# Lists of two numbers a token, weights gathered from a table, and list work dealt out by estimated time

## The chip, the cores and the metric

The kernel runs on one core of a Trainium2 chip. The metric is the device time in microseconds (us) of one execution, the median over runs. The engines of the core work side by side, each through its own instructions in order: TensorE (PE, matrix products into PSUM), VectorE (DVE), ScalarE (ACT), GpSimd (POOL), and SyncE (SP), which here issues most of the DMAs. An instruction that waits for a semaphore holds all that stand behind it on its engine.

## The reference

The first half is linear attention with decay over 4 batches, 8 heads, 768 positions and head size 64. Its output, as a matrix x of 3072 tokens by 512, goes through a mixture of 8 experts of which each token takes the two best:

```
logits = x @ w_gate;  noisy = logits + log1p(exp(x @ w_noise)) * noise
top2 = the two largest of noisy (8 experts);  w = softmax over these two
out[token] = sum over its two experts e of  w * (relu(x @ w1[e]) @ w2[e])    # 512 -> 1024 -> 512
```

All is float32.

## The kernel before

**Attention.** A loop over `t` from 0 to 11 takes two chunks of 128 tokens a turn (a stage, "stage t"). In it PE transposes k and q of the next pair (`trans_k`, L297; `trans_q`, L310), makes the state products (`kv`, L385), the outputs of pair t (`intra`, `inter`, L350), transposes earlier outputs (`store_x`, L413), multiplies them with the gate's weights (`products`, L404) and makes the scores of the next pair (`scores`, L338), then the logits (L429). ACT empties most of the PSUM results: kT, qT, xo (`evac_o`), xc (`store_x`) and xp (`products`). DVE makes qTs (L317), the states S (L397) and the masked scores `at` (L341). POOL makes kd (`kdecay`, L326). The PSUM name pS has four slots; a stage takes twelve of them in turn (three for k, two for q, one for kv, two for xc, four for the scores), so the third and fourth of the scores take the slots of the two xc.

**Routing.** The tokens are routed in three groups of eight chunks (`GB`). `gate` finds the two best experts of each token (DVE), `weights` their softmax (POOL, the reciprocal on DVE), `count` counts tokens per expert with small PE products of the one-hot `ob`, and `route` gives each choice a place: a tile number `at` and a row `lo` in it.

**Lists.** For each chunk and choice a list unit holds two one-hot codes: `lo` (128 wide, the row) and `hi` (56 wide, the tile; L577). `loads` multiplies hi by the five numbers that a token carries in `vals` (two for its index, three bfloat16 pieces of its weight; L588). `enlist` multiplies lo by that on PE (L598) and adds the result to `found`: for each expert's tile and row, the token's index and weight. `read_lists` and `decode` turn a part of `found` into `recs` (index and weight), and `gather_rows` fetches rows of x from DRAM by an indirect DMA of POOL (L772).

**Order of the work.** Each engine's order is the order of the program's text. Gate, weights, count, route and parts of the lists are generators in `jobs`; `advance(n)` steps through them, a step counting 1 unless it yields another number, and "step" ends the call. In attention it is called after the state updates (`FILLS`) and at the end of a stage (`FILL`, less `SPLIT` where weights are split). The first six units of two chunks are built outright at the end of a stage, at most two a stage (`firsts`, `UPS`), as soon as their group is routed; the list call follows at the end of the next stage.

**Experts.** For expert 0, tiles of 128 tokens go in three parts of 2, 2 and 3 tiles: GEMM1 over eight blocks f (L797, `gemm1`), evacuated by ACT (relu, L803) and DVE (L807), and GEMM2 per tile (L835, `gemm2`), whose result is multiplied by the token's weight (L850, L847). The lists of groups 1 and 2 are finished inside the first two parts; `MIDS` runs something after 12 of the 24 matmuls of a tile. Weights are loaded by SP to `wst` and split in a high and a low part (`split_w`, ACT L748 and DVE L749). Each expert's results are scattered to the output by POOL (L854), after fetching what an earlier expert wrote there (`gather_prev`, L819).

Of the kernel before, what the change touches and what calls it, by code (L numbers as in the profile page):

```python
# [55 lines left out]
NV = 5  # L56
HOT = 2 * (128 + NTL + NV * NTL)
UPS = 2
# [4 lines left out]
FILL, SPLIT, FILLS = 10, 4, 14  # L63
FILL1 = 4
FILL2 = (7, 7, 7, 3, 3, 3, 3, 3)
# [5 lines left out]
GX = 9  # L71
# [53 lines left out]
def kernel(  # L125
# [16 lines left out]
    x_tok = dram.tile([NTOK, DM], FT, name="x_tok")  # L142
    powd = dram.tile([H, 2, 256], FT, name="powd")
# [93 lines left out]
    nc.gpsimd.iota(iotat, pattern=[[1, NTL]], base=0, channel_multiplier=0, allow_small_or_imprecise_dtypes=True)  # L237
    iotar = consts.tile([128, TS], BF, name="iotar")
    nc.gpsimd.iota(iotar, pattern=[[1, TS]], base=0, channel_multiplier=0, allow_small_or_imprecise_dtypes=True)
    vals = consts.tile([128, NCH, 2, NV], BF, name="vals")  # L240
    nc.gpsimd.iota(vals[:, :, :, 0], pattern=[[1, NCH], [0, 2]], base=-(BIG // TS), channel_multiplier=0,
                   allow_small_or_imprecise_dtypes=True)
    nc.gpsimd.iota(vals[:, :, :, 1], pattern=[[0, NCH], [0, 2]], base=0, channel_multiplier=1,
# [32 lines left out]
    def finish(b):  # L276
        while "done" not in RT.get(b, {}):
            advance(1)
# [153 lines left out]
    def gate(b):  # L432
# [18 lines left out]
        acc = t(fl, "glacc")  # L451
# [8 lines left out]
        nl = t(sh, "nl")  # L460
# [23 lines left out]
    def weights(b):  # L484
# [19 lines left out]
        w = t([128, gs, 2], "ww")  # L504
        v.tensor_copy(w[:, :, 0], s)
        v.tensor_mul(w[:, :, 1], e, s)
        cs = slice(GB[b], GB[b + 1])
        for i in range(2, NV - 1):
            v.tensor_copy(vals[:, cs, :, i], w)
            v.tensor_tensor(vals[:, cs, :, i + 1] if i == NV - 2 else w, w, vals[:, cs, :, i], op=SUB)  # L510

# [12 lines left out]
    def route(b):  # L524
# [24 lines left out]
        v.scalar_tensor_tensor(pp, ei, float(NT * TS), pp, op0=MULT, op1=ADD)
# [4 lines left out]
        v.tensor_scalar(atr, pp, 1.0 / TS, -0.5 + 0.5 / TS, op0=MULT, op1=ADD)  # L554
# [16 lines left out]
    def keys(b, c, n, buf):  # L571
# [3 lines left out]
        for o, io, x in ((lo, iotar, RT[b]["lo"]), (hi, iotat, RT[b]["at"])):  # L575
# [4 lines left out]
            yield  # L580
# [28 lines left out]
    def decode(s, out, n):  # L609
# [36 lines left out]
    def places(b):  # L646
        yield "step"
# [537 lines left out]
```

## Time and profile before

| | us |
|---|---|
| median of 3 runs | 780.5 (779.52 to 782.52) |
| the profiled execution | 778.15 |
| its span, first to last instruction | 776.4 |
| PE busy | 733.4 |
| DVE, ACT, POOL busy | 361.4, 223.0, 235.8 |

The span is the time between the first and the last instruction; the profiled execution takes 1.75 us more. An engine's busy time is no measure of its importance by itself: what counts is which wait ends last before an instruction of PE. PEclk is the clock that PE was granted, as a share of 2.4 GHz; 0.5 is 1.2 GHz.

### The profile page before, as it was taken

To read this page: it belongs to the slowest core of one execution; us is meant where nothing else is said; L and a number is where in the kernel's file an instruction comes from. 1 tells how busy PE (TensorE), PEld (TensorE's weight loads), DVE (VectorE), ACT (ScalarE), POOL (GpSimd) and SP (SyncE) were. 2 spreads that over 40 slices of the span, in tenths; PEclk is the share of its full clock that TensorE was granted. 3 is DMA by queue.
4 is the path that set the end of the run, shared out by engine and by line. 5 is a ranking of instruction groups with operands and counts; after the bars stand their busy time and mean duration, and the time that the engine had idled before them with its cause. 6 is when DMAs were issued, how large, how long until landed. Compare 5 with 4: busy or idle time off the path is not lost. (4 is left out here: it accounts for less than half of the span.)

```text
span 776.4 us, 15432 instructions
## 1 busy us (share of the span) xinstructions
PE 733.4 (94%) x6170; PEld 625.6 (81%) x6170; DVE 361.4 (47%) x820; ACT 223.0 (29%) x381; POOL 235.8 (30%) x383
## 2 busy tenths in 40 slices
PE   6999996969989999999999999999999999999995
PEld 4887885858869889898888888888798888889884
DVE  5555788749643554454235333623352443335210
ACT  0445553423203332133213221422142222314200
POOL 2311431302252344332343343243412433221311
PEclk9899999889989999999999999999999999999998
DMA  8899983319063473534253425333442544240210
GB/s 169 190 275 225 280 202 112 123 49 338 1 160 120 137 197 100 178 113 134 86 151 125 123 75 170 123 110 107 142 144 68 155 137 135 66 136 12 75 41 37
DMA packets 88924, 103.21 MB, mean 133 GB/s; under 512 B 35462, under 2 KB 61574, under 8 KB 88848
## 3 DMA queue, kind: packets, MB, share of 16 engines
q1 hardware_dynamic: 77280, 66.01, 31.8%
q0 software_dynamic: 11568, 36.17, 14.3%
q8 instruction: 50, 0.82, 0.4%
q14 instruction: 26, 0.21, 0.1%
HBM read 77.73 MB, written 25.64 MB: 133 GB/s over the span
## 5 line engine op out<-in xcount | busy, mean ns | idle before, releaser
L797 PE MATMUL pS<-xtl,w1h 128*128 128x512 f32 (+3 forms) x544 | 181.9, 334 | 6.2 <-DVE xtl L784 6.1
L797 PE MATMUL pS<-xth,w1h 128*128 128x512 f32 (+3 forms) x544 | 182.6, 336 | 2.8 <-ACT xth L783 2.5
L797 PE MATMUL pS<-xth,w1l 128*128 128x512 f32 (+3 forms) x544 | 181.5, 334 | 0.0
L807 DVE SCALAR_TENSOR_TENSOR ht<-pS,ht 128x256 fp32r<-128x256 f32 (+3 forms) x176 | 76.7, 455 | 136.3 <-ACT ht L803 134.3
L835 PE MATMUL pO<-w2h,ht 128*128 128x512 f32 x384 | 126.2, 400 | 0.0
L835 PE MATMUL pKV<-w2h,ht 128*128 128x512 f32 x384 | 124.8, 396 | 0.0
L803 ACT ACTIVATE ht<-pS 128x512 fp32r<-128x512 f32 (+3 forms) x136 | 65.8, 484 | 184.7 <-PE pS L797 180.2
L854 POOL DMA_INDIRECT out_dram<-ot,rec x46 | 60.5, 1315 | 186.1 <-DVE ot L847 175.2
L797 PEld LDWEIGHTS pS<-xtl,w1h 128*128 128x128 f32 x544 | 103.8, 191 | 15.4 <-DVE xtl L784 6.8
L797 PEld LDWEIGHTS pS<-xth,w1h 128*128 128x128 f32 x544 | 103.4, 190 | 12.6 <-ACT xth L783 3.3
L797 PEld LDWEIGHTS pS<-xth,w1l 128*128 128x128 f32 x544 | 103.5, 190 | 8.8
L783 ACT ACTIVATE xth<-pS 128x512 fp32r<-128x512 f32 (+2 forms) x53 | 29.9, 573 | 208.6 <-PE pS L781 208.5
L835 PEld LDWEIGHTS pO<-w2h,ht 128*128 128x128 f32 x384 | 72.9, 190 | 15.6
L835 PEld LDWEIGHTS pKV<-w2h,ht 128*128 128x128 f32 x384 | 72.1, 188 | 15.5
L835 PE MATMUL pO<-w2l,ht 128*128 128x512 f32 x192 | 75.7, 394 | 0.0
L835 PE MATMUL pKV<-w2l,ht 128*128 128x512 f32 x192 | 75.1, 391 | 0.0
L819 POOL DMA_INDIRECT pv<-out_dram,rec x46 | 46.8, 1018 | 29.2 <-issue 26.0
L772 POOL DMA_INDIRECT xg<-x_tok,rec x46 | 49.0, 1065 | 17.0 <-issue 16.1
L847 DVE SCALAR_TENSOR_TENSOR ot<-pO,rec,pv 128x512 f32<-128x512 f32 x21 | 15.8, 751 | 81.1 <-PE pO L835 81.1
L847 DVE SCALAR_TENSOR_TENSOR ot<-pKV,rec,pv 128x512 f32<-128x512 f32 x21 | 15.8, 751 | 79.8 <-PE pKV L835 79.8
L326 POOL TENSOR_TENSOR kd<-kt,Mk 128x512 f32<-128x512 f32 x24 | 26.6, 1130 | 77.0 <-PE pR L385 41.4
L749 DVE TENSOR_TENSOR w2l<-wst,w2h 128x1024 fp32r<-128x1024 f32 (+1 forms) x33 | 39.4, 1193 | 13.3 <-ACT w2h L748 13.3
(214 smaller groups left out, 971.8 us busy)
## 6 DMA issues: line engine op xcount, KB each, us to landing
wst<-in_moe_w_dram SPq DMA_DIRECT2D x48, 512.0 KB, 4.0
wst<-in_moe_w_dram SPq DMA_DIRECT2D x32, 256.0 KB, 3.8
kt<-in_k_dram SPq DMA_DIRECT2D x12, 512.0 KB, 5.7
qt<-in_q_dram SPq DMA_DIRECT2D x24, 256.0 KB, 6.4
vt<-in_v_dram SPq DMA_DIRECT2D x12, 512.0 KB, 6.2
x_tok<-xc SPq DMA_DIRECT2D x24, 256.0 KB, 4.3
out_dram<-zero SPq DMA_DIRECT2D x24, 256.0 KB, 4.1
xg<-x_tok,rec POOLq DMA_INDIRECT x46, 4.0
```

The costliest lines, as they stand in the source:

```text
L326: nc.gpsimd.tensor_mul(kd[:, :, s], kt[:, :, s], mask(s, slice(0, HP), slice(C - 1, C)).to_broadcast([128, HP, 2, D]))
L749: nc.vector.tensor_tensor(lo[:, r], st[:, r], hi[:, r].bitcast(FT), op=SUB)
L772: nc.gpsimd.indirect_dma_start(out=XG[t][:size(e, t)], out_offset=None, in_=x_tok[:rows, :], in_offset=bass.IndirectOffsetOnAxis(ap=REC[e, ...
L783: nc.scalar.activation(hi, p, AF.Copy)
L797: nc.tensor.matmul(p, W1[a][d][:, fs], xt(b, cs)[:, d], start=(d == 0 and i == 0), stop=(d == DB - 1 and i == 2))
L803: nc.scalar.activation(ht(e, 0, f, cs), p, AF.Relu)
L807: nc.vector.scalar_tensor_tensor(ht(e, 1, f, c), p[:, r], 0.0, ht(e, 0, f, c).bitcast(FT), op0=OP.max, op1=SUB)
L819: nc.gpsimd.indirect_dma_start(out=PV[t][:size(e, t), :], out_offset=None, in_=out, in_offset=bass.IndirectOffsetOnAxis(ap=REC[e, t][:, 0: ...
L835: nc.tensor.matmul(p, ht(e, a, f, cs), W2[b][f // 2][:, f % 2, :], start=(i == 0), stop=(i == len(terms) - 1))
L847: nc.vector.scalar_tensor_tensor(o, p, w, pv, op0=MULT, op1=ADD)
L854: st = nc.gpsimd.indirect_dma_start(out=out, out_offset=bass.IndirectOffsetOnAxis(ap=REC[e, t][:, 0:1], axis=0), in_=o, in_offset=None, bo ...
```

## The change

A token's list entry becomes two numbers, chunk and row, so `NV` is 2 and a unit is 592 columns a chunk instead of 928. `loads` no longer reads `vals`: DVE writes hi times the chunk number, one instruction a chunk, and ACT writes hi times the row number (`scale=rowf`). `weights` no longer writes three pieces; POOL spreads the two weights over the experts and writes them to a table `wtab` in DRAM (token by expert). `decode` gives a token's index and the place of its weight in the table, and `gather_w`, a new indirect DMA on POOL for each tile, fetches the weights to `WR`. `route` drops three steps.

`advance` now counts estimated microseconds: a step counts `OPUS` = 0.21 unless it yields its own estimate. All allowances change. The units are no longer built outright: `build(early(b))` is a job behind `routing(b)`, four units for group 0 (four buffers `HB`) and two for group 1. The first tiles' lists are read as soon as group 0 is listed, not at t = 9. In expert 0, the lists of group 1 are called one block earlier (f = 5), and the counting of group 2 is moved from the middle of tile 1's GEMM2 to the end of tile 0's.

```diff
-NV = 5
+NV = 2
...
-FILL, SPLIT, FILLS = 10, 4, 14
-FILL1 = 4
-FILL2 = (7, 7, 7, 3, 3, 3, 3, 3)
+OPUS = 0.21
+FILL, SPLIT, FILLS = 2.0, 1.2, 3.4
+FILL1, FILLG = 0.9, 4.6
...
-                n -= j or 1
+                n -= j or OPUS
...
             v.max(mx[:, c, :], nl[:, c, :])
-            yield
+            yield 0.1
...
             v.max_index(mi[:, c, :], mx[:, c, :], nl[:, c, :])
-            yield
+            yield 0.15
...
-        w = t([128, gs, 2], "ww")
-        v.tensor_copy(w[:, :, 0], s)
-        v.tensor_mul(w[:, :, 1], e, s)
...
+        wd = t([128, 2, gs, E], "wd")
+        v.tensor_mul(e, e, s)
+        for i, w in enumerate((s, e)):
+            v.tensor_mul(wd[:, i], r["oh"][:, i], w[:, :, None].to_broadcast(sh))
+        v.tensor_add(wd[:, 0], wd[:, 0], wd[:, 1])
+        nc.gpsimd.dma_start(wtab.rearrange("(p c) o -> p (c o)", p=128)[:, GB[b] * E:GB[b + 1] * E],
+                            wd[:, 0].rearrange("p c e -> p (c e)"))
...
-            yield
+            yield 0.0012 * 2 * n * k + 0.08
...
-        v = nc.vector
         _, hi, mv = hot(buf, n)
-        sh = [128, 2 * n, NV, NTL]
-        g = GB[b] + c
-        v.tensor_tensor(mv.rearrange("p k (w j) -> p k w j", w=NV), hi[:, :, None, :].to_broadcast(sh),
-                        vals[:, g:g + n].rearrange("p c r w -> p (c r) w")[:, :, :, None].to_broadcast(sh), op=MULT)
+        mv = mv.rearrange("p k (w j) -> p k w j", w=NV)
+        nc.scalar.activation(mv[:, :, 1, :], hi, AF.Copy, scale=rowf)
+        for i in range(n):
+            k = slice(2 * i, 2 * i + 2)
+            nc.vector.tensor_scalar(mv[:, k, 0, :], hi[:, k, :], float(GB[b] + c + i - BIG // TS), None, op0=MULT)
...
+    def gather_w(e, t):
+        n = size(e, t)
+        nc.gpsimd.indirect_dma_start(
+            out=WR[e % 3][:n, t:t + 1], out_offset=None, in_=wtab,
...
     def build(some):
-        for unit in some:
-            yield from keys(*unit)
-            loads(*unit)
-            yield
+        for b, c, n, buf in some:
+            yield from keys(b, c, n, buf)
+            loads(b, c, n, buf)
+            built.append((b, c, n, buf))
+            yield 0.36
+
+    def early(b):
+
+        return [(b, 2 * i, 2, x) for i, x in enumerate(HB[:4 if not b else 2])]
...
         if 2 * t in GB[1:]:
-            jobs.append(routing(GB.index(2 * t) - 1))
+            b = GB.index(2 * t) - 1
+            jobs.extend((routing(b), build(early(b))))
...
-        while len(built) < UPS and firsts and "done" in RT.get(firsts[0][0], {}):
-            b, c = firsts.pop(0)
-            built.append((b, c, 2, HB[c // 2 % 2]))
-            for _ in build(built[-1:]):
-                pass
-        if t == GX:
-            assert RT[0]["listed"] == GM
+        if RT.get(0, {}).get("listed") == GM and not REC:
             read_lists(0, PARTS0[0])
             load_rec(0)
             for j in range(PARTS0[0]):
                 gather_rows(0, j, GB[1] * C)
+                gather_w(0, j)
...
-    MIDS = {1: lambda: advance(1), 2: lists_done}
+    MIDS = {2: lists_done}
...
-                if f == 6:
+                if f == 5:
                     enlist(units[1])
...
-            advance(50)
+            advance(FILLG)
...
             gemm2(0, t, MIDS.get(t))
+            if t == 0:
+                finish(2, "gated")
+                advance(FILLG)
...
                         gather_prev(e, f)
+                        gather_w(e, f)
```

## Rows read from the trace of the kernel before

**Rows 1.** The head of the page: busy us, share of the span and instructions.

```profile
PE 733.4 (94%) x6170; PEld 625.6 (81%) x6170; DVE 361.4 (47%) x820; ACT 223.0 (29%) x381; POOL 235.8 (30%) x383
```

**Rows 2.** Busy time by stretch, cut at the starts of the attention stages t = 7, 8, 9, 10 and at later points; columns: stretch, its length, busy us of PE, PEld, DVE, ACT and POOL, granted clock, DMA share, GB/s.

```profile
97.80:107.97 10.17, 10.17 (x238) 9.01 (x235) 7.21 (x25) 6.03 (x11) 3.28 (x8) 1.00 0.81 196
107.97:122.39 14.42, 11.43 (x266) 9.90 (x266) 12.19 (x19) 5.20 (x10) 2.78 (x2) 1.00 0.85 231
122.39:141.29 18.90, 13.91 (x267) 11.83 (x266) 16.72 (x45) 6.35 (x11) 3.14 (x2) 0.82 0.17 57
141.29:151.23 9.94, 9.94 (x234) 8.85 (x233) 8.28 (x43) 6.03 (x11) 5.38 (x16) 1.00 0.35 110
151.23:166.94 15.71, 7.05 (x135) 5.28 (x134) 11.30 (x27) 4.75 (x9) 3.64 (x13) 0.90 0.18 67
166.94:196.88 29.94, 28.29 (x187) 25.45 (x188) 18.56 (x83) 7.46 (x17) 5.94 (x20) 0.94 0.68 246
196.88:231.11 34.23, 29.26 (x181) 25.14 (x180) 20.91 (x53) 5.63 (x13) 11.27 (x19) 0.95 0.29 78
231.11:770.00 538.89, 536.04 (x2760) 456.32 (x2760) 207.65 (x346) 142.02 (x227) 174.22 (x248) 1.00 0.38 116
```

**Rows 3.** PE's waits over the whole span: what waited, for whom, total us, times, longest.

```profile
PE pS L797 <- DVE xtl L784: 6.1, 2, 5.7
PE pS L413 <- DVE qTs L317: 3.4, 1, 3.4
...
PE pR L404 <- DVE S L397: 2.2, 1, 2.2
PE pL L598 <- DVE wst L588: 2.2, 2, 2.0
...
PE pL L598 <- DVE l L439: 1.4, 1, 1.4
...
PE pS L338 <- ACT xc L415: 0.8, 2, 0.5
```

**Rows 4.** DVE's timeline at the end of stage t = 7 (start us, us, what), two list units and the qTs behind them; the last row is POOL's at that time.

```profile
109.64 0.68 DVE L577 TENSOR_TENSOR hb<-iotar,lo 128x512 bf16<-128x512 bf16 x1
110.24 0.38 DVE L577 TENSOR_TENSOR hb<-iotat,at 128x224 bf16<-128x224 bf16 x1
110.73 1.32 DVE L588 TENSOR_TENSOR hb<-hb,vals 128x1120 bf16<-128x1120 bf16 x1
111.97 1.54 DVE L577 TENSOR_TENSOR hb<-iotar,lo 128x512 bf16<-128x512 bf16 x1
113.43 1.23 DVE L577 TENSOR_TENSOR hb<-iotat,at 128x224 bf16<-128x224 bf16 x1
...
115.94 0.68 DVE L317 TENSOR_TENSOR qTs<-pS,QS 128x512 f32<-128x512 f32 x1
...
111.64 2.78 POOL L326 TENSOR_TENSOR kd<-kt,Mk 128x512 f32<-128x512 f32 x2 [3.83 <-issue]
```

**Rows 5.** Timelines of stage t = 7: DVE's last routing instruction, then ACT, then PE's scores.

```profile
103.98 0.20 DVE L502 RECIPROCAL ws<-ws 128x8 f32<-128x8 f32 x1
...
103.51 0.60 ACT L372 ACTIVATE xo<-pO 128x512 f32<-128x512 f32 x1 [2.18 <-PE pO L350]
...
104.48 1.09 ACT L415 ACTIVATE xc<-pS 128x512 f32<-128x512 f32 x2
105.44 0.41 ACT L406 ACTIVATE xp<-pR 128x256 f32<-128x256 f32 x1
...
104.97 2.06 PE L338 MATMUL pS<-qT,kT 64*64 64x128 f32 x63
```

**Rows 6.** The end of attention: DVE's weight split and the low part of expert 0's first rows, ACT's high part, and PE.

```profile
159.87 1.23 DVE L749 TENSOR_TENSOR w2l<-wst,w2h 128x1024 fp32r<-128x1024 f32 x1 [1.89 <-ACT w2h L748]
...
165.61 1.28 DVE L784 TENSOR_TENSOR xtl<-pS,xth 128x512 fp32r<-128x512 f32 x2
...
159.73 1.09 ACT L783 ACTIVATE xth<-pS 128x512 fp32r<-128x512 f32 x2
...
166.94 0.58 PE L797 MATMUL pS<-xtl,w1h 128*128 128x256 f32 x1 [5.69 <-DVE xtl L784]
```

**Rows 7.** The first part of expert 0: ACT's first evacuation, and DVE's last gate instruction of group 2.

```profile
174.65 0.66 ACT L803 ACTIVATE ht<-pS 128x256 fp32r<-128x256 f32 x2 [2.44 <-DMA x_tok<-xc]
...
193.22 0.23 DVE L480 TENSOR_TENSOR ob<-oh 128x64 bf16<-128x64 f32 x1
```

**Rows 8.** Busy time by stretch, as in Rows 2, of a stretch in stage t = 9.

```profile
133.00:140.00 7.00, 5.75 (x90) 4.64 (x90) 6.35 (x24) 1.70 (x3) 0.00 (x0) 0.52 0.37 115
```

**Rows 9.** Groups of instructions over the span: line, engine, operation, shapes, count, busy us, mean ns, idle before.

```profile
L598 PE MATMUL pL<-hb 128*128 128x280 bf16 x24 | 3.3, 282 | 0.0
...
L577 DVE TENSOR_TENSOR pv<-iotat,at 128x112 bf16<-128x112 bf16 x4 | 1.1, 268 | 0.0
...
L772 POOL DMA_INDIRECT xg<-x_tok,rec x46 | 49.0, 1065 | 17.0 <-issue 16.1 <-DMA wst<-in_moe_w_dram 0.3 <-PE pS L781 0.3
```

**Rows 10.** PE's timeline at the last list call and at the transposes that wait for the third gather.

```profile
213.74 1.13 PE L598 MATMUL pL<-wst 128*128 128x280 bf16 x8
...
217.69 0.64 PE L598 MATMUL pL<-wst 128*128 128x280 bf16 x4 [1.96 <-DVE wst L588]
...
230.18 0.46 PE L781 MATMUL pS<-identf,xg 64*128 64x64 f32 x4 [1.13 <-DMA xg<-x_tok,recs]
```

More of the change, by code (lines that the diff above doesn't have):

```diff
@@ L142 @@
     x_tok = dram.tile([NTOK, DM], FT, name="x_tok")
+    wtab = dram.tile([128 * NCH * E, 1], FT, name="wtab")
     powd = dram.tile([H, 2, 256], FT, name="powd")
@@ L236 @@
     iotat = consts.tile([128, NTL], BF, name="iotat")
[L237 removed]
+    nc.gpsimd.iota(iotat, pattern=[[STRIDE // TS, E], [1, NT]], base=0, channel_multiplier=0,
+                   allow_small_or_imprecise_dtypes=True)
     iotar = consts.tile([128, TS], BF, name="iotar")
     nc.gpsimd.iota(iotar, pattern=[[1, TS]], base=0, channel_multiplier=0, allow_small_or_imprecise_dtypes=True)
[L240 to L241 removed]
+    rowf = consts.tile([128, 1], FT, name="rowf")
+    nc.gpsimd.iota(rowf, pattern=[[0, 1]], base=-TS, channel_multiplier=1, allow_small_or_imprecise_dtypes=True)
+    tokb = consts.tile([128, NCH, NV], BF, name="tokb")
+    nc.gpsimd.iota(tokb[:, :, 0], pattern=[[1, NCH]], base=-(BIG // TS), channel_multiplier=0,
                    allow_small_or_imprecise_dtypes=True)
[L243 removed]
+    nc.gpsimd.iota(tokb[:, :, 1], pattern=[[0, NCH]], base=-TS, channel_multiplier=1,
+                   allow_small_or_imprecise_dtypes=True)
+    WBASE = (BIG // TS) * E + TS * NCH * E
+    wcol = consts.tile([128, E, NT], FT, name="wcol")
+    nc.gpsimd.iota(wcol, pattern=[[1, E], [0, NT]], base=WBASE, channel_multiplier=0,
                    allow_small_or_imprecise_dtypes=True)
@@ L273, in advance, with finish @@
             else:
-                n -= j or 1
-    def finish(b):
-        while "done" not in RT.get(b, {}):
-            advance(1)
+                n -= j or OPUS
+    def finish(b, what="done"):
+        while what not in RT.get(b, {}):
+            advance(0.01)
     qT, qTs, kT, KD, AT, XO, XP, PO, SA, first, KV = [{} for _ in range(11)]
@@ L607, in enlist, with decode @@
             RT["found"] = True
-    def decode(s, out, n):
+    def decode(s, out, n, base):
         v = nc.vector
@@ L676 @@
     EXP = {0: slice(0, 1)}
-    HB = [ac.tile([128, 2 * HOT], BF, name=f"hb{i}") for i in range(2)]
+    HB = [ac.tile([128, 2 * HOT], BF, name=f"hb{i}") for i in range(4)]
+    WR = [rp.tile([128, NT], FT, name=f"wr{i}") for i in range(3)]
+    for x in WR:
+        nc.gpsimd.memset(x, 0.0)
     N1 = E - 1
@@ L927 @@
                 gather_rows(0, j, GB[1] * C)
+                gather_w(0, j)
         if t in LOADS:
             load_w(LOADS[t][0], 0, LOADS[t][1])
+        if t == 3:
+            nc.sync.dma_start(wtab.rearrange("(p c) o -> p (c o)", p=128), zero[:, :NCH * E])
         if t == 2:
             nc.sync.dma_start(nz, sub(noise, 0, [[E, 128], [128 * E, NCH], [1, E]]))
+    assert REC
+    finish(1)
+    advance(50)
     for j in range(2):
@@ L937 @@
     store_x(NST - 1)
-    assert not firsts and len(built) == UPS
     enlist(built)
+    built.clear()
     head.append(mm1(0, 0, PARTS0[0], 1))
@@ L964, in lists_done @@
             gather_rows(1, j)
-    MIDS = {1: lambda: advance(1), 2: lists_done}
+        for j in range(4, 7):
+            gather_w(0, j)
+    MIDS = {2: lists_done}
     for i, (t0, n) in enumerate(parts(0)):
@@ L988 @@
                 zero_out(3)
-                advance(FILL2[f])
+                advance(FILL1)
             if i == 2 and f >= 4:
@@ L1024 @@
     ovt = rp.tile([128, 3, MAXOV], FT, name="ovt")
+    ovw = rp.tile([128, MAXOV], FT, name="ovw")
     tab = rp.tile([128, MAXOV], I32, name="tab")
@@ L1114 @@
         e_r = nc.sync.value_load(tab[0:1, bass.ds(it, 1)], min_val=0, max_val=E - 1)
-        row = rp.tile([128, 1], FT, name="row")
+        row, base = [rp.tile([128, 1], FT, name=nm) for nm in ("row", "base")]
         nc.sync.dma_start(row, ovi[:, bass.ds(it, 1)])
+        nc.sync.dma_start(base, ovw[:, bass.ds(it, 1)])
         away = rp.tile([128, 2, NCH], FT, name="away")
@@ L1122 @@
             nc.vector.tensor_scalar(key, iotar, away[:, i, c:c + 1], None, op0=OP.is_equal)
-            nc.tensor.matmul(pl[:, :NV], key, vals[:, c, i, :], start=not j, stop=(j == len(pairs) - 1))
+            nc.tensor.matmul(pl[:, :NV], key, tokb[:, c, :], start=not j, stop=(j == len(pairs) - 1))
         rt = rp.tile([128, 1, RW], I32, name="reco")
```

58 lines of the change are left out of this document (25 added, 33 removed).

## The prediction

> **What bounds the kernel now.** I read the head of the page first [rows 1]: TensorE (PE) is busy for 733.4 us of a span of 776.4, VectorE (DVE) for 361.4. PE is the bound, so the question is where PE stands idle or runs at the lower clock. The busy time by stage [rows 2] answers the first: from 231.11 to 770 PE is busy 536.0 of 538.9 us, and nothing can be won there. Five stretches between 107.97 and 231.11 hold 3.0 + 5.0 + 8.7 + 1.7 + 5.0 = 23.3 us of idle. The waits [rows 3] name DVE for most: 6.1 us for xtl, 3.4 for qTs, 2.2 for list units in wst, 1.4 for the copy l. What DVE does meanwhile stands in its timeline [rows 4]: after the masks of stage t=8's scores it builds two list units before it turns to the qTs that the next stage needs. The granted clock answers the second [rows 8]: from 133 to 140 it is 0.52, nearly the whole stretch at 1.2 GHz instead of 2.4, after PE had waited 3.4 us for qTs [rows 3].
>
> **The change, part by part.** I follow the planner's new numbers (an unmarked step 0.21, stage allowances 3.4 and 2.0 or 0.8, `FILL1` 0.9, `FILLG` 4.6) through the loops and put durations of the rows in.
>
> *A unit.* Before: lo 0.68, hi 0.38, product 1.32 us of DVE [rows 4]. After: lo and hi the same, two DVE products of 128x112 by a constant, and one ScalarE (ACT) pass of 128x224. No row shows these. The nearest DVE row is a 128x112 compare of 0.27 us [rows 9] and, from below, nothing at all; I take 0.15 each, as a one-operand pass should be no longer than the two-operand compare. For ACT the nearest row is 0.41 us for 128x256 [rows 5]; between nothing and 0.41 I take 0.35, near that row. A list matmul has 112 columns for 280: 3.3 us/24 = 0.14 each before [rows 9]; between 0 and 0.14 I take 0.06 by columns.
>
> *The wait that is added.* The ACT pass reads hi, so it waits for DVE, and everything behind it on ACT waits too. Behind it stand the evacuations that PE needs.
>
> *Stage t=7 (97.80).* DVE does what it did up to the reciprocal (to 104.2, as before [rows 5]), and now also lo and hi of unit 0 (to 105.2), its products and lo of unit 1 (to 106.1, just when the masks are due, so DVE costs nothing itself). But ACT's pass stands ahead of the evacuation xo, which began at 103.51; it now begins at 105.55, xc follows to 107.75 instead of 105.57. The second half of the scores writes the two PSUM slots that xc empties; PE came there about 105.9, half way through its 2.06 us [rows 5], and now waits to 107.75: 1.85 us lost. (That PE can wait for xc here is in [rows 3]: 0.8 us, twice.) With a first list of 0.25 the stage ends at 110.0 instead of 107.97.
>
> *Stage t=8.* hi of unit 1 comes after the weight split on DVE, at 111.75; ACT's pass waits for it ahead of kT, which starts at 112.1 instead of about 110.75. PE loses 1.0 us at the transposes. Three more products and compares fill DVE until 118.7; the last ACT pass holds xo to 118.8, xc is ready at 121.0, and the scores lose 1.65 us. Twelve list matmuls end at 123.6. The stage that took 14.42 us [rows 2] takes 13.6, for the two builds before qTs are gone: half of what they cost comes back as ACT's wait. So after t=8 the new kernel stands 1.2 us behind.
>
> *Stage t=9.* Before, 18.90 us: two builds, then routing, then PE at 1.2 GHz. After, no build at all is left; routing has 17 steps of about 0.23, 3.9 us, which delays the masks by 1.3 and the following transposes by 0.6. Undisturbed stages take 10.17 and 9.94 us [rows 2], so I take 10.9: gain 8.0.
>
> *Stages 10, 11 and the first expert rows.* The count matmuls only move. One list call of 0.25 is added. At the end, before: DVE split the weights (159.87, 1.23 us), built two units and reached xtl at 165.61 [rows 6]; PE went on at 166.94. After: split to 161.1, hi of one unit to 161.35, ACT's pass to 161.75, and behind it xth, which began at 159.73, to 162.85; xtl ends at 163.6. Gain 3.4, less 0.25: 3.2.
>
> *First part of expert 0 (from the end of the last store, 171.36 before, called 0 here).* The first ht evacuation still waits for a store to land, at 3.3 [rows 7]. Then each of four small units makes ACT and DVE wait for each other in turn (ht, split, hi, ACT pass): I add their rows one behind the other and the fourth is ready at 11.6. The list call is now ahead of the seventh GEMM1 block; PE gets there at 7.45 and waits 4.15 us. Before, it waited 1.4 behind that block. gemm2 of tile 0 so ends at 20.4 for 19.5. The counting of group 2 now follows that tile at once instead of in the middle of the next. Its input ob came at 193.45, 22.1 on this clock [rows 7]; the four big products are gone from DVE's queue but lists come one block earlier and nothing overtakes, so I get 22.85. PE waits 2.5 us at the count, with tile 1 of gemm2 behind it. Tile 1 ends at 28.95 instead of 25.5: loss 3.4.
>
> *Lists of expert 0's last tiles.* All units are built some 5 us before the call, so the 2.2 us of waiting go, and 16 matmuls take 1.0 us instead of 2.1. From the last list matmul (218.33) to the third gather's rows (230.18) is 11.9 us [rows 10], table, gather and queue; this chain stays, less 0.2 for a shorter table. PE has 36 matmuls of 0.23 and two tiles of transposes, 9.3 us, before it needs those rows, so it now waits 2.4 us for them where it waited 1.13 (and part of its way went at the lower clock). From the start of the call (213.74) to the rows were 16.4 us; now 1.1 + 11.7 = 12.8. Gain 3.6.
>
> *Weight gathers.* 53 more on POOL, each about 1.0 us like the row gathers [rows 9], whatever their bytes, and 0.3 between; at most 70 us on an engine busy 235.8 of 776 [rows 1]. In a GEMM1 step of 512 columns (12 matmuls of 0.23, 2.75 us) stand a spacer 0.18 and two gathers, 2.8 us: seven steps overrun by half a microsecond, and the eighth has none. The weights are needed a gemm2 tile later. Cost 0; if the cover were gone, 1.3 us for each of seven experts, 9. Writing the table (three small POOL transfers and some products) and one more zero fill: 0, beside PE.
>
> *Sum.* -2.05 + 0.8 + 8.0 + 3.2 - 3.4 + 3.6 = 10.2 us off the span. I charge 1 us for the clock: the new waits in t=7 and t=8 may be followed by a stretch at 1.2 GHz as the waits of stage t=9 were. That is 9 us: the profiled execution would go from 778.15 (span 776.4 and 1.75 around it) to about 769, and the median, which lies 2.35 above the profiled one, from 780.5 to 771.5.
>
> **Rivals.**
> *ACT holds nothing* (the evacuations have more slack than I read, or hi comes earlier). Then t=7 and t=8 take 10.4 and 10.9, a gain of 3.3 instead of -1.25; expert 0's first part loses 1.5 instead of 3.4: 17 us, 763.5. For it: PE waited for xc only 0.8 us in all [rows 3]. Against it: ACT's order in the code, and 105.2 against 103.51.
>
> *The estimates miss what POOL does to DVE.* The planner has one price for lo, 0.69; the rows show 0.68 and, beside POOL's kd at 111.64, 1.54, and 1.23 for hi instead of 0.38 [rows 4]. If that meets the products and compares of t=7 and t=8, about seven instructions at 0.86, the ACT waits lengthen by as much: 6 us, and 777.5 is left. Against it: by my times kd runs beside the state updates there. The Trainium skill (Advanced Engine Details and Errata, VectorE Performance Modes) says that two-port Vector instructions and GpSimd block each other, since they share a port; a one-operand bf16 product within SBUF fits its conditions for two ports. The trace agrees that the two engines slow each other, by the lo and hi above, though these have two operands.
>
> *Slower: the new waits bring the lower clock.* Each of the four waits that I add (t=7, t=8, list call, count) would have to be followed by 6.8 us at 1.2 GHz in which PE is the bound, 3.4 each, as from 133 to 140 [rows 8]: 13.6 us on 771.5 are 785. It decides from the third such stretch on. Against it: the wait at the count shrinks when PE is late, and the 2.2 us for S in t=8 [rows 3] were followed by none: the whole of t=8 shows clock 1.00 [rows 2].
>
> **How the numbers follow.** My forecast has 0.50, ACT holding nothing 0.25, the contention 0.15, the slower case 0.10. About 0.5% (3.9 us) is what can be told from no change. The forecast's own range is 767 to 776, so nearly all of it is faster by that much; with the second case and a third of the contention that is 0.77; same 0.14, slower 0.09. The range from 763 to 780 leaves out a fifth: the best of the second case, the worst of the third, and the last.
>
> **What would show it.** After: t=9 at 10.5 to 11.5 us and full clock (the largest term). xo in t=7 beginning behind an ACT pass, at 105 or later; PE waiting for ACT xc in the scores of t=7 and t=8. xtl at about 163 on the old clock. PE waiting for ob at the count of group 2, and for units at the list call. No wait for wst, a longer one for xg. POOL with 53 more gathers of 1 us. I am wrong if t=9 still takes over 14 us, or if PE has idle time past 240.

## The result, and the profile after

The changed kernel took 792.87 us (median of 4 runs, 789.62 to 794.09) beside 781.51 for the kernel before: ratio 1.0134, 95% interval 1.0085 to 1.0183. I had forecast 771.5 us, and at most 780. The profiled execution took 789.62 (span 787.7). Its head and its busy time by stretch, cut as in [rows 1, 2] at the starts of t = 7 to 10, then at the first GEMM1 matmul after the attention, at those of the second and third part of expert 0 and of expert 1, and at the last matmul:

```profile
PE 740.5 (94%) x6170; PEld 627.1 (80%) x6170; DVE 348.5 (44%) x823; ACT 227.8 (29%) x395; POOL 289.4 (37%) x438
```

```profile
95.66:107.45 11.79, 10.82 (x243) 9.25 (x239) 9.48 (x27) 6.39 (x12) 4.83 (x7) 1.00 0.77 185
107.45:120.94 13.49, 11.23 (x273) 9.42 (x269) 8.95 (x24) 6.30 (x13) 2.06 (x2) 1.00 0.74 200
120.94:138.07 17.13, 14.91 (x261) 11.73 (x257) 13.16 (x45) 6.47 (x11) 6.19 (x6) 0.80 0.35 106
138.07:159.28 21.21, 16.82 (x371) 14.16 (x370) 16.31 (x62) 11.52 (x22) 7.32 (x26) 0.99 0.26 92
159.28:197.60 38.32, 32.04 (x193) 28.76 (x193) 22.85 (x105) 10.20 (x24) 10.88 (x30) 0.83 0.53 193
197.60:228.60 31.00, 25.66 (x172) 22.42 (x172) 11.94 (x35) 6.14 (x15) 10.25 (x11) 0.98 0.39 101
228.60:265.40 36.80, 35.65 (x188) 31.33 (x188) 12.94 (x28) 9.94 (x18) 10.67 (x16) 0.93 0.34 107
265.40:774.27 508.87, 508.34 (x2574) 426.70 (x2572) 193.59 (x319) 131.56 (x210) 209.61 (x278) 1.00 0.38 114
```

Stages t=7 and t=8 (11.79, 13.49) are close to the forecast; t=9, the largest term, took 17.13 instead of 10.9, at clock 0.80, and over 14 us there was my own sign of being wrong. The last row is one that my sum held to be fixed. PE's waits, which answer to [rows 3], and the late starts of ACT's evacuations behind 231 us:

```profile
PE pL L599 <- DVE l L445: 4.5, 1, 4.5
PE pS L809 <- ACT xth L795: 4.1, 2, 3.4
...
PE pS L344 <- ACT xc L421: 2.1, 2, 1.2
...
PE pS L316 <- ACT kT L305: 1.0, 1, 1.0
...
PE pL L522 <- DVE ob L486: 0.8, 1, 0.8
```

```profile
ACT ht L815 <- issue: 22.7, 11, 2.1
ACT ht L815 <- remote: 21.1, 6, 5.1
```

The first block holds the waits that I had forecast, at the forecast places: the list call 4.5 (forecast 4.15), kT 1.0 (1.0), xc 2.1 in all (3.5), ob 0.8 (2.5). The second holds what I had not: six times ACT stood for up to 5.1 us before an evacuation whose signal, of PE, the profile could not place (a late signal, below). In the trace of before there are none such. ("issue" and "remote" are the profile's words for waits that it can put down to no instruction of the core.)

**A pair to read the change from.** Single executions differ by where PE falls to 1.2 GHz, so I compare two profiles from one later job (e13, the kernel before; e16, the changed one, both below) that lost the same to the low clock up to 300 us: 15.4 us each, summed over half microseconds as one minus the granted clock. First e13, then e16, cut alike:

```profile
99.09:109.07 9.98, 9.98 (x239) 8.89 (x235) 7.01 (x24) 6.03 (x11) 3.25 (x8) 1.00 0.81 197
109.07:123.68 14.61, 11.41 (x266) 9.88 (x266) 12.38 (x19) 5.20 (x10) 3.00 (x3) 1.00 0.80 232
123.68:142.74 19.06, 14.07 (x266) 11.99 (x265) 16.73 (x45) 6.35 (x11) 3.14 (x2) 0.82 0.18 57
142.74:200.30 57.56, 46.37 (x563) 40.42 (x561) 39.41 (x154) 19.34 (x39) 15.74 (x52) 0.94 0.47 166
200.30:232.80 32.50, 28.22 (x172) 24.30 (x172) 19.63 (x51) 4.54 (x11) 10.54 (x15) 0.95 0.29 77
232.80:266.70 33.90, 33.80 (x189) 30.50 (x189) 13.15 (x28) 10.06 (x18) 9.28 (x15) 0.95 0.46 135
266.70:768.93 502.23, 502.23 (x2574) 425.76 (x2572) 193.85 (x318) 131.98 (x210) 163.90 (x232) 1.00 0.38 115
```

```profile
96.52:108.32 11.80, 10.83 (x243) 9.25 (x239) 9.28 (x27) 6.40 (x12) 4.83 (x7) 1.00 0.76 187
108.32:121.81 13.49, 11.23 (x273) 9.42 (x269) 8.95 (x24) 6.30 (x13) 2.06 (x2) 1.00 0.72 203
121.81:135.16 13.35, 10.12 (x261) 8.93 (x257) 12.30 (x44) 6.20 (x11) 6.21 (x6) 0.97 0.48 154
135.16:197.10 61.94, 51.02 (x560) 44.95 (x560) 40.15 (x167) 21.95 (x45) 18.16 (x56) 0.84 0.41 146
197.10:226.70 29.60, 25.73 (x173) 22.49 (x173) 12.00 (x35) 6.14 (x15) 9.11 (x10) 1.00 0.35 91
226.70:260.50 33.80, 33.80 (x188) 30.29 (x188) 13.10 (x28) 10.05 (x18) 11.79 (x17) 0.95 0.44 128
260.50:768.05 507.55, 507.55 (x2574) 426.81 (x2572) 193.94 (x319) 131.99 (x210) 209.63 (x278) 1.00 0.38 114
```

When expert 1 begins, the changed kernel is 6.2 us ahead (260.50 against 266.70). Then it loses 5.3 us in a stretch in which both run the same matmuls at full clock with PE never idle, and 4.4 us behind the last matmul (the tail): the spans end at 778.1 and 781.6, 9.2 and 13.6 us after it. The next rows show where. POOL's scatters of the last tiles of 24 matmuls, in e13 and in e16, start 5.49 and 5.62 us apart:

```profile
759.01 0.98 POOL L854 DMA_INDIRECT out_dram<-ot,rec  x1 [4.43 <-DVE ot L847]
764.50 0.98 POOL L854 DMA_INDIRECT out_dram<-ot,rec  x1 [4.43 <-DVE ot L847]
```

```profile
757.87 0.98 POOL L866 DMA_INDIRECT out_dram<-ot,rec  x1 [4.58 <-DVE ot L859]
763.49 0.98 POOL L866 DMA_INDIRECT out_dram<-ot,rec  x1 [4.58 <-DVE ot L859]
```

And the program's last line: POOL's queue has three DRAINs there (times in ns, shortest, median and longest). The longest comes after the last scatter and takes 3.18 us in e13 and 7.67 in e16, and SP's longest wait at that line grows by as much, from 3.5 to 8.0 us. First e13, then e16:

```profile
L1181 POOLq DRAIN  x3: 46/103/3180, 774.1 to 777.8; - x3
SPq L1181 <- PEq L1181: 4.1, 2, 3.5
```

```profile
L1206 POOLq DRAIN  x3: 46/103/7672, 773.1 to 781.3; - x3
SPq L1206 <- PEq L1206: 8.6, 2, 8.0
```

### The profile page after: what moved, and what is told of

It reads as the page before. It is cut to its first block, busy times and chain, and to the rows that moved or that the text cites. A ratio compares the mean times of both kernels' runs of the same rounds, so it can differ in the third digit from the quotient of the medians.

```text
span 787.7 us, 15593 instructions
## 1 busy us (share of the span) xinstructions
PE 740.5 (94%) x6170; PEld 627.1 (80%) x6170; DVE 348.5 (44%) x823; ACT 227.8 (29%) x395; POOL 289.4 (37%) x438
## 4 chain that ended last, share of the span: by engine, by line
PE 81%; issue 6%; DVE 3%; ACT 3%; DMA 2%; another core or an unknown queue 2%; POOL 1%; SPq 1%; ACTq 0%; POOLq 0%; DVEq 0%
PE pS L809 33%; PE pKV L847 15%; PE pO L847 14%; PE pS L793 3%; PE pS L344 3%; PE pO L356 2%; PE pKV L356 2%; PE pS L303 2%; PE pS L419 1%; PE pO L852 1%; PE pS L391 1%; PE pS L316 1%; DMA QS<-powd 1%; PE pKV L852 1%
## 5 line engine op out<-in xcount | busy, mean ns | idle before, releaser
L809 PE MATMUL pS<-xth,w1h 128*128 128x512 f32 (+3 forms) x544 | 184.8, 340 | 6.0 <-ACT xth L795 4.1
L809 PEld LDWEIGHTS pS<-xth,w1h 128*128 128x128 f32 x544 | 105.2, 193 | 16.3 <-ACT xth L795 4.8
L831 POOL DMA_INDIRECT pv<-out_dram,rec x46 | 47.1, 1023 | 16.9 <-issue 13.6
L784 POOL DMA_INDIRECT wr<-wtab,rec x46 | 45.9, 997 | 16.0 <-issue 15.1
L859 DVE SCALAR_TENSOR_TENSOR ot<-pKV,wr,pv 128x512 f32<-128x512 f32 x21 | 15.8, 751 | 79.9 <-PE pKV L847 79.9
L859 DVE SCALAR_TENSOR_TENSOR ot<-pO,wr,pv 128x512 f32<-128x512 f32 x21 | 15.8, 751 | 79.7 <-PE pO L847 79.7
L332 POOL TENSOR_TENSOR kd<-kt,Mk 128x512 f32<-128x512 f32 x24 | 24.8, 1057 | 64.2 <-PE pR L391 27.5
```

Source lines behind the costliest of these rows:

```text
L332: nc.gpsimd.tensor_mul(kd[:, :, s], kt[:, :, s], mask(s, slice(0, HP), slice(C - 1, C)).to_broadcast([128, HP, 2, D]))
L784: nc.gpsimd.indirect_dma_start(out=WR[e % 3][:n, t:t + 1], out_offset=None, in_=wtab, in_offset=bass.IndirectOffsetOnAxis(ap=REC[e, t][:, ...
L809: nc.tensor.matmul(p, W1[a][d][:, fs], xt(b, cs)[:, d], start=(d == 0 and i == 0), stop=(d == DB - 1 and i == 2))
L831: nc.gpsimd.indirect_dma_start(out=PV[t][:size(e, t), :], out_offset=None, in_=out, in_offset=bass.IndirectOffsetOnAxis(ap=REC[e, t][:, 0: ...
L859: nc.vector.scalar_tensor_tensor(o, p, w, pv, op0=MULT, op1=ADD)
```

## The experiments

The experiments ran in five jobs (e1 to e4, e5 to e8, e9 to e12, e13 to e16, e17 and e18), each on one chip beside the kernel before; e9 to e12, e17 and e18 had the same chip, the other three jobs three other ones. All ratios are to the kernel before in the same job, with 95% intervals. "Pace" is the time from the first to the last start of a full second-GEMM tile of 24 matmuls, the mean over the 43 or 44 such tiles from 240 us on; it was 5.337 us in the kernel before and 5.467 in the changed one, of which one tile of 6.32 us behind a late signal makes 0.02.

**e1, e2: 64-byte alignment.** Smaller buffers moved the expert weights by 800 bytes (672 come from `found`, 128 from `vals`, which smaller tables replace), `w2h0` from 56000 to 55200, 32 past a multiple of 64, and `ht` by 128. In e1 (changed kernel) and e2 (before) the edit is

```
+    padc = consts.tile([128, 8], FT, name="padc")     # ahead of W1, W2, XT, XG
+    padr = rp.tile([128, 8], FT, name="padr")         # ahead of okey
```

> The changed kernel with 32 unused bytes per partition ahead of the expert weights and 32 more behind their staging tiles, so that the weights start on a multiple of 64 bytes again, as they did before the change (the smaller found had moved them by 800 bytes), and all that lies behind stays where it was modulo 64. Theory A (the address of the operand makes the second GEMM slower): its matmuls start every 232 ns again instead of 237.8, a tile of 24 takes 5.36 us instead of 5.47, and the time falls by 6 to 7 us, from 792.9 to about 786. Rival B (the 53 weight gathers on POOL slow the second GEMM): 237.8 ns and 793, as without the padding.

> The kernel before with the same two paddings: here they move the expert weights from a multiple of 64 bytes to 32 past one, and nothing else of the kernel. Theory A: second-GEMM matmuls every 237 to 238 ns instead of 232, and 6 to 7 us more, 788. Rival B: 781.5, no change.

e1: 783.68 us, 1.0035 (1.0006 to 1.0064), pace 5.411. e2: 786.77 us, 1.0072 (1.0037 to 1.0107), pace 5.428. Theory A in this form is half wrong: the multiple of 64 bytes does not give the old pace back, yet moving tiles in the kernel before, with no instruction of its work changed, slows it.

**e3, e4: the gathers alone.** e3 adds 53 unused gathers to the kernel before; e4 takes them from the changed one.

```
                         gather_prev(e, f)
+                        gather_w(e, f)          # e3; in e4 the calls go, and WR is set to 0.5
```

> The kernel before with 53 more gathers of one number a token from a table of zeros, at the places where the changed kernel gathers its weights; nobody reads them. Theory C (the gathers cost at the end and in the first GEMM): the last DRAIN of POOL goes from 3.2 to 7.7 us and the tail behind the last matmul from 9.2 to 13.4; ACT's ht evacuations begin late by some us in places; together 4 to 6 us more, about 786.5, with the second GEMM at 232 ns. Rival B: the second GEMM too goes to 237.8 ns, and the time to about 792. Rival D (gathers are hidden, as I predicted): 781.5.

> The changed kernel without its weight gathers: the routing weights are left out, each is the constant 0.5. Theory A and C together: the tail is 9.2 us again and the late evacuations are gone, 4 to 6 us less (787 to 789), while the second GEMM stays at 237.8 ns; stage t=9, which has two gathers less between its first matmuls, loses part of its 17.1 us. Rival B: the second GEMM returns to 232 ns, and the time to about 781. Rival D: 793.

e3: 789.24 us, 1.0112 (1.0067 to 1.0158); tail 13.1 us, DRAIN 7.43, no late evacuation, pace 5.428. e4: 777.63 us, 0.9963 (0.9927 to 0.9998), 10 us below what I expected; tail 9.3 us, DRAIN 3.42, pace 5.445. The DRAINs of e3 and e4:

```profile
L1199 POOLq DRAIN  x3: 46/103/7427, 780.0 to 788.0; - x3
...
L1200 POOLq DRAIN  x3: 46/103/3425, 769.4 to 773.4; - x3
```

The tail is the gathers': DRAIN grows by 4.25 us for 53 of them and by 0.24 for the three table writes that e4 keeps, 0.08 us for each added POOL DMA both times, and 56 make the 4.49 of the changed kernel. The pace is not theirs in e4, so B falls there; in e3 the gathers' buffers had also moved `ht` by 128 bytes, and e17 tells the two apart.

**e5, e6: how much is the execution?** No edit.

> The kernel before, unchanged, for a second profile: how much of a difference between two single profiles is the execution and not the kernel. If the pace of the second GEMM belongs to the kernel (theory A), a tile of 24 matmuls has 5.34 us from first to last start again and the stretch from expert 1's first GEMM to the last matmul 502 us; if it belongs to the execution (theory E), it comes out elsewhere between 5.33 and 5.47.

> The changed kernel, unchanged, beside the others of this job. Theory A: 5.47 us a tile. Theory E: anywhere between 5.33 and 5.47. The tail behind the last matmul is 13.4 us by both. Time: 1.008 to 1.018 of the kernel before.

e5: 782.72 us, 1.001 (0.9992 to 1.0029), pace 5.337. e6: 784.30 us, 1.0030 (1.0006 to 1.0054), pace 5.445, tail 13.6 us, no late evacuation. The pace belongs to the program. But the same program that had measured 1.0134 is here 1.0030, below the 1.008 to 1.018 that I expected: some 8 us of the recorded result come and go with the job.

**e7: no gathers, and aligned.** The edits of e1 and e4 together.

> The changed kernel without its weight gathers (each routing weight is the constant 0.5) and with the expert weights on a multiple of 64 bytes. If the two causes are apart and add up: 5 to 7 us below the run without gathers alone, so 0.987 to 0.990 of the kernel before, about 771 to 773, which is where my prediction stood. If the alignment is nothing: 0.996, as without gathers alone.

776.53 us, 0.9942 (0.992 to 0.9965), pace 5.411, as in e1. The alignment is worth the difference of pace, 0.034 us for 44 such tiles, under 2 us: a miss for "5 to 7".

**e8: ScalarE's pass.**

```
-        nc.scalar.activation(mv[:, :, 1, :], hi, AF.Copy, scale=rowf)
+        nc.vector.tensor_scalar(mv[:, :, 1, :], hi, rowf, None, op0=MULT)
```

> The changed kernel with the second list product on VectorE in place of ScalarE, so that no ScalarE pass waits for VectorE's hi. Theory (the ScalarE pass holds the evacuations behind it): PE's waits for ACT xc (0.9 and 1.2 us), kT (1.0) and xth (3.4) go or shrink, VectorE gets 0.2 us more work a unit; 2 to 5 us less than the changed kernel, 1.004 to 1.011 of the kernel before. Rival (what ScalarE gives back VectorE takes, since masks and qTs come later): no change beyond 1 us.

776.59 us, 0.9942 (0.9895 to 0.9988), 7.7 us below e6 in the same job, more than the 2 to 5 that I expected. Stages t=7 and t=8 take 10.38 and 11.80 us (e6: 11.80 and 13.49), the wait at the list call 2.2 (4.8), for ACT xth 1.3 at most (3.4), and up to 300 us 10.2 us go to the low clock instead of 13.7. The passes on ScalarE cost about what lay between my forecast and my rival "ACT holds nothing" (8 us), part of it as low clock.

**e9, e10: the old places.** Two routing buffers go ahead of the expert weights with 128 unused bytes, so that `w1h0`, `w2h0`, `xth0`, `wst`, `ht` and the expert tiles behind have the addresses of the kernel before. e10 adds the edit of e8.

```
-        ohp = t([128, 2, gs, E], "ohp")
+        ohp = consts.tile([128, 2, gs, E], FT, name="ohp")
-    ovw = rp.tile([128, MAXOV], FT, name="ovw")
+    ovw = consts.tile([128, MAXOV], FT, name="ovw")
+    padc = consts.tile([128, 32], FT, name="padc")
```

> The changed kernel with two buffers of the routing moved ahead of the expert weights and 128 unused bytes, so that the expert weights, their staging tiles, ht and all behind it stand at the very addresses of the kernel before. Theory A (the place of the tiles in on-chip memory sets the pace of the second GEMM, finer than a multiple of 64 bytes tells: the paddings moved ht too): a tile of 24 has 5.34 us again instead of 5.445, and expert 1 to the last matmul 502.3 us instead of 507.5; 0.996 to 0.997 of the kernel before, about 779. Rival (the pace comes from the changed instructions): 5.445 and 1.003, about 784.

> The same with the second list product on VectorE. If the two add up: 7 to 8 us less than with the places alone, 0.987 to 0.988 of the kernel before, about 772. If the places change nothing: 0.994.

The pace is 5.338 in e9 and 5.337 in e10: the old one, with all changed instructions in place, and expert 1 to the last matmul takes 503.1 and 503.0 us. e9: 785.65 us, 1.0042 (1.0017 to 1.0066); e10: 778.35 us, 0.9949 (0.9918 to 0.998). The ratios missed what I expected. This job was one with late signals again, as e12 beside them shows: against its 1.0111 the places gave 0.7%, 5.4 us, and the products another 7.3.

**e11: the weights ride in the rows.** `x_tok` gets eight numbers a row, the token's weight for each expert; `w1h0`, `w2h0`, `xth0` and `ht` lie as in e9, products as in e8.

```
-    x_tok = dram.tile([NTOK, DM], FT, name="x_tok")
+    x_tok = dram.tile([NTOK, XW], FT, name="x_tok")       # XW = DM + E
...
-        nc.gpsimd.dma_start(wtab.rearrange("(p c) o -> p (c o)", p=128)[:, GB[b] * E:GB[b + 1] * E],
-                            wd[:, 0].rearrange("p c e -> p (c e)"))
+        nc.gpsimd.dma_start(x_tok.rearrange("(c p) w -> p c w", p=128)[:, GB[b]:GB[b + 1], DM:], wd[:, 0])
...
+        o, x = WR[e % 3][:n, t:t + 1], XG[t][:n, DM:XW]      # take_w, called by trans_rows
...
+        nc.vector.tensor_mul(wpick[:n], x, (mine[:n, e - 1, :] if e > 0 else mine[:n, N1, :]))
+        nc.vector.tensor_reduce(o, wpick[:n], axis=AX.X, op=ADD)
...
-                        gather_w(e, f)
```

> The same (old places, products on VectorE), and the weights reach the experts without gathers of their own: a row of x_tok has eight numbers more, the token's weight for each expert, the row gather brings them, and VectorE picks the expert's one with two small instructions a tile. If the closing DRAIN of POOL grows by 0.08 us for each POOL DMA (4.25 us for 53 gathers, 0.24 for three table writes): the tail is 9.4 us instead of 13.5, and 4 us go, 0.982 to 0.983, about 768. If the picks or the longer rows cost VectorE or the gathers what the tail gives: 772.

768.18 us (767.36 to 769.49), 0.9819 (0.9786 to 0.9852): faster than both kernels. It gains 10 us on e10, not 4: no evacuation of ht waits for a late signal here, and its four executions lie within 2.2 us, where the ten of e10 lie within 10.4; that the other 6 us are late signals is not shown by itself. The tail is 10.5 us, not 9.4 (DRAIN 4.98 for as many POOL DMAs as e4 had; why it is longer was not tried). The picks (0.16 us each) lie in DVE's gaps. Its stretches t=7 to t=9, and expert 1 to the last matmul:

```profile
99.44:110.10 10.66, 10.55 (x243) 9.21 (x239) 9.33 (x28) 6.03 (x11) 3.92 (x6) 1.00 0.83 202
110.10:121.69 11.59, 10.99 (x272) 9.42 (x269) 10.36 (x27) 5.09 (x10) 3.61 (x4) 1.00 0.97 253
121.69:134.41 12.72, 11.41 (x260) 9.41 (x258) 10.60 (x42) 6.31 (x11) 4.21 (x4) 1.00 0.44 138
253.90:756.14 502.24, 502.24 (x2574) 425.81 (x2572) 203.51 (x401) 131.95 (x210) 164.39 (x232) 1.00 0.39 116
```

**e12: the changed kernel, a third job.**

> The changed kernel unchanged, in a third job. Two jobs gave 1.0134 and 1.0030 of the kernel before. If the first was a matter of its chip: 1.002 to 1.006 and no ACT ht that waits for a late signal behind expert 0. If it belongs to the kernel and comes now and then: some executions of 789 us or more, with such waits of 4 to 5 us.

791.62 us, 1.0111 (1.0078 to 1.0145). The late signals are back, seven of them before ht. In ACT's, PE's and POOL's timelines (start us, us, what) one is seen whole, from the last of the twelve matmuls that the evacuation waits for; the last rows are busy times by stretch:

```profile
236.02 0.31 PE L809 MATMUL pS<-xth,w1l 128*128 128x320 f32 x1
...
239.39 0.99 POOL L866 DMA_INDIRECT out_dram<-pv,recs  x1 [0.21 <-issue]
...
240.69 0.99 POOL L866 DMA_INDIRECT out_dram<-pv,recs  x1 [0.21 <-issue]
...
242.25 0.31 PE L809 MATMUL pS<-xth,w1l 128*128 128x320 f32 x1 [1.67 <-issue]
...
243.67 0.44 ACT L815 ACTIVATE ht<-pS 128x320 fp32r<-128x320 f32 x1 [10.91 <-remote]
...
245.06 0.43 PE L809 MATMUL pS<-xtl,w1h 128*128 128x320 f32 x1 [1.68 <-issue]
```

```profile
240.00:242.30 2.30, 0.63 (x5) 0.56 (x5) 0.00 (x0) 0.00 (x0) 1.85 (x5) 1.00 0.42 171
242.50:250.00 7.50, 5.43 (x22) 5.21 (x21) 2.13 (x8) 1.89 (x5) 0.54 (x2) 0.54 0.13 55
```

ACT idles for 10.91 us. The twelfth matmul started at 236.02 and the evacuation only at 243.67, 7.6 us later, where e16 has 0.3 (229.92 and 230.26). Meanwhile POOL issues indirect DMAs 1.3 us apart, matmuls within one group stand for 1.7 us on nothing that the profile knows, and 7 us at half the clock follow. That the third part of expert 0 began at 232.8 and ended at 273.0, 40.2 us for the 33.8 of e16, is this. POOL's same burst is in e16 (232.55 to 237.47 us) without any of it.

**e13 to e16: gathers and late signals, in one job.** The kernels of e5, e3, e4 and e6.

> The kernel before beside the next three, in one job. If the late signals come only where weight gathers stand (theory L): no ACT ht that waits for a late signal behind expert 0, on whatever chip; 1.00.

> The kernel before with 53 gathers of one number that nobody reads, again. On a chip that shows late signals: some with the gathers, and 1.015 to 1.02 of the kernel before (1.0112 without them, in the first job). On a chip that shows none: 1.010 to 1.013. Rival (late signals belong to the changed lists, not to gathers): none here while the changed kernel beside it has them.

> The changed kernel without its weight gathers (each routing weight is the constant 0.5), again. Theory L: no late signals even where the changed kernel beside it has them, and 0.995 to 0.998 of the kernel before on any chip. Rival: late signals here too, and 1.003 or more.

> The changed kernel unchanged, beside the three. On a chip with late signals 1.010 to 1.014, with four or more ACT ht waits for them of 4 to 6 us; on a chip without them 1.002 to 1.006.

1.0012 (0.9983 to 1.0041), 1.0129 (1.0063 to 1.0194), 0.9953 (0.9928 to 0.9978) and 1.0040 (1.0011 to 1.0070). This job showed no late signal at all, so the test that I had hoped for did not come off. Over all profiles, late signals to ACT ht stand in four, the recorded one, e9, e10 and e12: each has weight gathers, and they come from two jobs. The other profiles with gathers (e1, e3, e6, e8, e14, e16), from three jobs, have none, and neither has any without gathers, e11 in the job of e12 among them. But late signals to other instructions stand in e11, e17 and e18 too, without weight gathers: all six profiles from the chip of e9 to e12 have some (the recorded job's chip is not known), and the twelve from three other chips have none. In e11 and e18 DVE's state update S waits 0.9 us in stage t=9. In e17, the kernel before but for 128 bytes, it is ACT's xth, and PE behind it stands for 3.94 us, where e13 has 0.47:

```profile
236.11 0.38 ACT L785 ACTIVATE xth<-pS 128x256 fp32r<-128x256 f32 x1 [1.53 <-remote]
...
236.54 0.64 PE L799 MATMUL pS<-xth,w1h 128*128 128x320 f32 x1 [3.94 <-ACT xth L785]
```

So a late signal does not need the weight gathers; with them, on the chip that shows it, there are more.

**e17: `ht` 128 bytes later.** The kernel before with `padr` of 128 bytes ahead of `okey`, and nothing else.

> The kernel before with 128 unused bytes ahead of the routing buffers: the weights keep their addresses, ht and all behind it stand 128 bytes later, as in the run with 53 unused gathers; no gather is added. Theory A (places set the pace): 5.43 us a tile of the second GEMM, as there, instead of 5.34, expert 1 to the last matmul 506 us instead of 502.3, and 1.004 to 1.006 of the kernel before. Rival (there the gathers slowed the second GEMM): 5.34 and 1.000.

786.95 us, 1.0048 (1.0021 to 1.0074), pace 5.428; from expert 1's first matmul to the last:

```profile
271.10:776.99 505.89, 505.89 (x2574) 425.36 (x2572) 193.82 (x318) 131.79 (x210) 163.89 (x232) 1.00 0.38 115
```

505.89 us for 502.23, with no gather, no other instruction than one memset of the unused bytes and the same busy times on DVE, ACT and POOL: the place alone. It explains e3's pace too, where the buffers had moved `ht` as far.

**e18: e11 with the list call one block later** (`if f == 6` for `if f == 5`).

> The kernel with the weights in the rows, and the list call of expert 0's first part behind the seventh block of the first GEMM, as before the change, instead of the sixth. Theory (the call waits for VectorE's units, and a stretch at half the clock follows): its wait of 2.3 us goes, at 172 to 176 us there is no half clock (1.7 us), 0.977 to 0.980 of the kernel before, 764 to 766. Rival (its rows then come later to the transposes): the wait for xg grows by as much, 0.982.

770.55 us, 0.985 (0.9822 to 0.9878), not faster than e11. The wait at the call falls from 2.3 to 1.1 us, but the one for ob at the count grows from 0.8 to 2.4, and the stretch at half the clock stands at 183.7 to 187.2 us instead of 172.6 to 176.0: the wait had only been moved.

## Why the prediction was wrong, point by point

The terms, from the pair e13 and e16 (plus is time lost):

| step | forecast | measured |
|---|---|---|
| t=7 | +2.05 | +1.8 |
| t=8 | -0.8 | -1.1 |
| t=9 to PE's first matmul on xtl in expert 0 | -11.2 | -6.6 |
| from there to expert 0's second part | +3.4 | +5.2 |
| second part | -3.6 | -2.9 |
| third part | 0 | -0.1 |
| expert 1 to the last matmul | 0 | +5.3 |
| tail | 0 | +4.4 |

Ahead of t=7 the changed kernel stood 2.6 us better, of which 1.7 is luck: a half-clock stretch at the start that was longer in e13.

*Right in kind, but not in size: the list steps.* From t=7 to expert 1 they gained 3.7 us, where my sum had 10.2. What I had said of ACT's pass came true. It stood before xo in t=7 and held it: xo began 7.6 us into the stage (forecast 7.75, before 5.7). The pass took 0.48 us (I took 0.35), a DVE product 0.19 (0.15). e8 prices the holding at 7.7 us.

*Mis-sized: "Stage t=9 ... Undisturbed stages take 10.17 and 9.94 us, so I take 10.9 ... full clock".* The two builds went, and PE's 3.4 us for qTs with them, but the masks behind the routing steps came later than the 1.3 us I allowed: in e16 PE waits 3.2 us for DVE's `at` at the next transposes, and stage t=9 takes 13.35. What I had put at nothing there is POOL beside DVE. In e16 the eight steps `gn` take 4.66 us, since one of them stands for 2.84 us instead of 0.23 and ends at 132.24, 0.1 us behind POOL's kd. The rows are of DVE's and POOL's timelines, of line 461 (shortest, median and longest of the eight steps in ns) and of PE's waits:

```profile
128.87 4.66 DVE L461 SCALAR_TENSOR_TENSOR gn<-gn,ge 128x64 f32<-128x64 f32 x8
L461 DVE SCALAR_TENSOR_TENSOR gn<-gn,ge x8: 224/226/2843, 128.9 to 133.3; 128x64 f32<-128x64 f32 x8
130.07 2.07 POOL L332 TENSOR_TENSOR kd<-kt,Mk 128x512 f32<-128x512 f32 x2
...
PE pS L303 <- DVE at L347: 3.2, 1, 3.2
```

With 0.23 there the masks could have begun 2.6 us earlier, PE would have waited 0.6 us, and t=9 would have taken about 10.7, an estimate from these rows and near my 10.9. Every profile of the changed lists has one such step in t=9: 2.0 to 2.9 us, and 1.0 in e11 and e18. In the recorded run, e9, e10 and e12 DVE's state update there also waits 1.6 us for a late signal, and t=9 takes 14.9 to 17.1 us, where e1, e6, e8 and e16 have 13.35 or 13.36. The clock did not return either: some 7 us at half of it still stand there in the recorded run (128 to 135 us) and at its end in e16 (134 to 141).

*The slower rival was half right.* Its mechanism shows at one of its four waits: behind the list call PE is at half the clock from 175 to 182 us in e16 and in the recorded run, 3.4 us, as priced, where e13 has none; the first part is 1.8 us worse than forecast. Right behind t=7, t=8 and the count there was none.

*The contention rival was right in kind and wrong in place.* lo of a unit took 0.64 to 0.69 us in t=7 and t=8, never 1.54: kd ran from 106.0 to 108.1 and from 113.2 to 115.3 in e16, and no compare met it. It was a routing step in t=9 that met kd, for 2.6 us.

*Wrong: "Weight gathers. ... Cost 0".* I looked for a price beside PE and found none. A small one is there: two gathers stand ahead of kd on POOL in t=9, and without them (e4, e7, e15) the slow step takes 2.0 us and t=9 12.54, 0.8 less. The large one is 4.4 us at the end, in an instruction of the program's last line that my sum had as a constant ("1.75 around it" and the tail inside the span). In some jobs more late signals come with them.

*Missing: the places.* My sum lists instructions, and "from 231.11 to 770 nothing can be won there" left 539 of 776 us out of it. That 2,574 matmuls with unchanged instructions could run more slowly was in no step. The smaller buffers are in the diff; what follows from them is 5.3 us, and in e11, with `w2` and `ht` where they were, the stretch has its 502.24 again. The Trainium skill (SBUF — State Buffer, the section on the two separate sides) says that only the port pair of Vector and GpSimd contends on the engines' side and that PE waits for nobody. It says nothing there on where an operand lies, and that counts here: e17 shows 5.428 for 5.337 us by 128 bytes, with no other engine busier.

Taken together, for this pair: ahead of t=7 -2.6, lists and stages -3.7 for the -10.2 of my sum, places +5.3, tail +4.4. That makes +3.4 us, where the medians give +0.3 to +0.4% (2 to 3 us) in two jobs without late signals (e6, e16). So three steps failed: the 10.9 us of t=9, "Cost 0" for the gathers, and the stretch held to be fixed. The recorded result lies some 8 us above that, and e12 some 6. Both have late signals, with half-clock stretches behind some of them. That these make up the whole is not shown: the recorded profile is 6.1 us longer than that of e16, and 4.2 of this lies behind the start of expert 0's third part. What decides whether late signals come, the chip or something else of the job, stays open.

## What to carry to other kernels

A change that shrinks or adds a buffer moves every tile behind it; compare the addresses of the big matmul operands before and after, and hold them, as one would hold a queue's order. Count what a DMA leaves to be closed at the end of the program, not only the engine time that it takes. Two engines that slow each other have to be priced beside every step of the sum, not only beside the new ones: POOL's kd met a routing step that was there before. And a small value that belongs to a row was cheaper here in the row (768.18 us for 778.35 with gathers of its own, e11 and e10): the gather that is paid already brings it.

## What the runs showed of the hardware that I had not expected

- The pace of 512-column fp32 matmuls whose moving operand is `w2` follows where `w2` and `ht` lie: 5.337 us a tile at (56000, 134784), 5.428 at (56000, 134912) and at (56032, 134848), 5.411 at (55232, 134720), 5.445 at (55200, 134656), the last without the two profiles (5.464, 5.467) in which a late signal held one tile. `wst` and `ot` at other places in e11 changed nothing (5.336). Matmuls of the first GEMM with 512 columns started every 227 ns in all of them. Which property of the addresses counts was not found.
- POOL's closing DRAIN: 3.18 us, then 3.42, 7.43 and 7.67 with 3, 53 and 56 more POOL DMAs. It is not the number alone: in e11, with 3 more and rows of 520 numbers instead of 512, it took 4.98.
- One DVE step on 128x64 fp32 with two operands took 2.84 us instead of 0.23 beside POOL's kd (e16), 2.0 to 2.9 in ten other profiles of the changed lists.
- A signal of PE reached ACT some 7 us late (e12: 7.6 us from the start of the last matmul to the evacuation, 0.3 in e16), and matmuls stood for 1.7 us, while POOL issued indirect DMAs every 1.3 us. Late signals stand in the recorded profile and in all six from one chip, with weight gathers and without, and in none of twelve from three other chips.
